# A new order for the attention's software pipeline ahead of two feed-forward blocks on Trainium2

## The chip, the core and the metric

The kernel runs on one core of one Trainium2 chip. The metric is device time in microseconds of one launch, median of three runs. The engines are named as the profile names them: PE (TensorE) with its weight loads PEld, DVE (VectorE), ACT (ScalarE), POOL (GpSimd) and SP (SyncE, which issues nearly all the DMAs).

## What is computed

Sliding-window attention with sink tokens, then two feed-forward blocks, all in float32:

```python
scores = scale * q @ k^T            # batch 2, heads 8, 768 tokens, head_dim 64
keep = (key < n_sink) | ((0 <= query - key) & (query - key < window))   # 4 and 128
a = softmax(where(keep, scores, -1e9))
x = (a @ v) as 1536 x 512
x = ((x @ w_a) * (x @ w_b)) @ w_out          # d_ff 1536
h = maximum(x @ w_in, 0); out = (h * h) @ w_out2   # d_ff 2048
```

The feed-forward weights arrive as 8-byte numbers of which the kernel itself makes float32, and every float32 product of the two blocks is made of three products of rounded parts (high times high, low times high, high times low).

## The kernel before

**Attention.** The work is cut into 24 groups: 2 batches, 6 blocks of 128 queries, 2 halves of 4 heads. A group passes through named stages, which the function `attention_fast` defines: `scores` (PE, L225), `soft0` and `soft1` (DVE, L238 and L241: fold the two key blocks, add the mask, take the extremum), `exp0` and `exp1` (ACT, L249), `rec` (DVE, L254 and L255: reciprocal of the sums), `norm`, `normA`, `normP` (the four heads' scaling, shared by DVE L259, ACT L264, POOL L269), `sp` (POOL, L278 to L280: the sink probabilities split in parts), `pst` and `ptp` (PE transposes, L310 and L286), `st` and `th` (ACT copies out of PSUM), `lu` (POOL, L301 and L303: two triangular parts), `x` (PE, L324 and L329: times the values), `xh` (ACT) and `xl` (DVE, L340), which leave the high and low part of the result in SBUF. A first block of a batch (`i == 0`) has no sinks and no second key block, so its groups are lighter.

The loop runs over 27 steps. In step g the table `ORDER` is gone through from left to right; an entry `(name, lag)` issues stage `name` of group g + lag. All four engines execute what they are given in that order (`manual_schedule`), so the table is each engine's instruction order.

**Beside the attention.** Three kinds of entry belong to the feed-forward part. `abs`, `ts`, `stt`, `stt2`, `cast`, `lo` are the six stages in which one weight matrix of 128 x 512 is decoded (method `Weights.stages`: ACT L511, DVE L515 and L516, DVE L519, DVE L522, ACT L527, DVE L529); the table `DECODE` says in which step the decoding of the j-th matrix starts, the lag of an entry moves its stage to a later step. `fill` issues the 12 PE products of one feed-forward piece (L619), `fu` and `fm` take its result out of PSUM (ACT L632, DVE L636). A piece is issued once 512 tokens of x are finished and, for the first eight, once its weights are decoded. The eight PSUM banks go to the scores (4), to the transposes and x (2), and to two more of the latter until step `WIDE`, when these two become the banks of the feed-forward pieces (pool `ps_a0`).

Ahead of the loop, `warm(WARM0)` issues 14 PE products of a zero matrix (L349), whose results nobody reads. `later_masks` (L116 to L124, six DVE operations) and `flag` (L131 to L136, five small ones, whose result is read after the whole fast path) stand behind step 0.

**After the attention.** The eight pieces that are left run with further decoding, then the pool `ps_a0` is closed and two new pools of four banks each are opened, `ps_y` for the accumulators (L660) and `ps_a` for the inner products (L619), and six phases over the remaining weights follow, each over three blocks of 512 tokens.

Of the kernel before, what the change touches and what calls it, by code (L numbers as in the profile page):

```python
# [16 lines left out]
PSUM = bass.MemoryType.PSUM  # L17
# [8 lines left out]
NRAW, AHEAD = 3, 2  # L26

ORDER = [
# [4 lines left out]
DECODE = [2, 5, 9, 10, 11, 12, 12, 15, 18, 20, 22]  # L33
WIDE = 9
VS = (3, 6)
PINNED = 3
WARM0 = 14
NQ, NV, NEX, NTH, NLU, NSP = 3, 5, 3, 2, 2, 2
NK = 4
T = 512  # L40
# [67 lines left out]
def out_of(v, o, x, limit):  # L108
    v.tensor_scalar(out=o, in0=x, scalar1=limit, scalar2=-BIG, op0=ALU.is_ge, op1=ALU.mult)


def later_masks(tc, cp, tp, c):
    v = tc.nc.vector
    m0, m1, m2 = c.m
    c.up = cp.tile([P, P], I32, name="upi")
    v.tensor_copy(c.up, c.upf)  # L116

    out_of(v, m2[:, 0:P], c.rel, c.w)
    v.tensor_copy(m2[:, P:SW], c.sink[:, 0:SK])

    t = tp.tile([P, P], F32, name="t")
    v.scalar_tensor_tensor(out=t, in0=c.col, scalar=c.ns, in1=c.upf, op0=ALU.is_lt, op1=ALU.mult)
    v.scalar_tensor_tensor(out=m1[:, 0:P], in0=t, scalar=-BIG, in1=m2[:, 0:P], op0=ALU.mult, op1=ALU.min)
    v.tensor_copy(m1[:, P:SW], c.sink[:, 0:SK])  # L124


def flag(tc, cp, c):

    v = tc.nc.vector
    f = cp.tile([P, 4], F32, name="flags")  # L130
    v.tensor_scalar(out=f[:, 0:1], in0=c.ns, scalar1=float(SK), scalar2=None, op0=ALU.is_gt)  # L131
    v.tensor_scalar(out=f[:, 1:2], in0=c.w, scalar1=float(P), scalar2=None, op0=ALU.is_gt)
    v.tensor_scalar(out=f[:, 2:3], in0=c.w, scalar1=1.0, scalar2=None, op0=ALU.is_lt)
    v.reduce_max(out=f[:, 3:4], in_=f[:, 0:3], axis=AX.X)
    c.slow = cp.tile([P, 1], I32, name="slow")
    v.tensor_copy(c.slow, f[:, 3:4])  # L136


def attention_fast(tc, ctx, c, cp, tp, q, k, v, vs_in, xh, xl, beside):
# [16 lines left out]
    def bank(name):  # L156

        turn[0] += 1
        return banks[turn[0] % len(banks)].tile([P, GH, P], F32, name=name, tag="tr")
# [34 lines left out]
    def sink_load(b):  # L194
        vsr[b] = p1.tile([96, H // 2, P], F32, name="vsr", tag="vsr")
        nc.sync.dma_start(vsr[b], vs_in[:, b])
# [30 lines left out]
    def maxima(g, pp):  # L227

        b, i, m = groups[g]
        if pp == 0:  # L230
            pns[g] = (p2.tile([P, GH, SW], F32, name="ex", tag="ex", bufs=NEX),
                      p2.tile([P, GH], F32, name="ss", tag="ss", bufs=NEX),
                      p2.tile([P, GH], F32, name="nb", tag="nb", bufs=NEX))
        ex, ss, nb = pns[g]
        w, at = (P, 0) if i == 0 else (SW, around(g)[1] * SW)
        sc = scs[g][pp]
        if i > 0:
            nc.vector.copy_predicated(sc[:, :, at:at + P], c.up.unsqueeze(1).to_broadcast([P, 2, P]),  # L238
                                      sc[:, :, SW - at:SW - at + P])
        for h in range(2 * pp, 2 * pp + 2):  # L240
            nc.vector.tensor_tensor_reduce(  # L241
                out=ex[:, h, 0:w], in0=sc[:, h % 2, at:at + w], in1=c.m[min(i, 2)][:, 0:w], scale=-0.125,
                scalar=3.0e38, op0=ALU.add, op1=ALU.min, accum_out=nb[:, h:h + 1])
# [100 lines left out]

    def warm(n):

        ps = bank("psw").rearrange("p h t -> p (h t)")[:, 0:2 * P]
        for _ in range(n):
            nc.tensor.matmul(ps, lhsT=beside.zero, rhs=beside.zero[:, 0:1].to_broadcast([P, 2 * P]), start=True,  # L349
                             stop=True)  # L350

    stages = dict(scores=scores, ptp=probs, th=probs_copy, lu=probs_select, soft0=lambda g: maxima(g, 0),
                  soft1=lambda g: maxima(g, 1), exp0=lambda g: exps(g, 0), exp1=lambda g: exps(g, 1), rec=reciprocal,
                  sp=sinks, pst=sinks_turn, st=sinks_copy, x=values, xh=x_high, xl=x_low,
                  norm=normalize, normA=normalize_a, normP=normalize_p)
    warm(WARM0)
    for g in range(N + 3):
        if g == WIDE:
            banks.pop()
            wide.close()  # L360
            beside.open()
        if g % 2 == 0:
            load_kq(g // 2 + 2)
            load_v(g // 2 + 1)
        if g == 0:
            sink_load(0)
        beside.fetch(g)
        for name, lag in ORDER:
            if name in stages:
                if 0 <= g + lag < N:  # L370
                    stages[name](g + lag)
            else:
                beside.stage(name, g + lag)
        if g == 0:
            later_masks(tc, cp, tp, c)
            flag(tc, cp, c)
        if g in VS:
            sink_split(VS.index(g))
            if g == VS[0]:
                sink_load(1)  # L380
# [177 lines left out]
class Beside:  # L558
# [18 lines left out]

    def fetch(self, step):

        if step + 1 in DECODE[:2]:  # L580
            self.W.load()

    def stage(self, name, step):
# [9 lines left out]
        else:  # L593
            for j, at in enumerate(DECODE):
                if at == step:
# [133 lines left out]
@with_exitstack  # L729
def sliding_window_moe_kernel(ctx, tc, q, k, v, vs, span, w_a, w_b, w_out, w_in2, w_out2, out):  # L730
    nc = tc.nc
    NT, DM = out.shape
    cp = ctx.enter_context(tc.tile_pool(name="cp", bufs=1))
    xp = ctx.enter_context(tc.tile_pool(name="xp", bufs=1))
    xh = xp.tile([P, DM // P, NT], F32R, name="xh")
    xl = xp.tile([P, DM // P, NT], F32R, name="xl")
    rp = ctx.enter_context(tc.tile_pool(name="rp", bufs=3))
    sa = ctx.enter_context(tc.tile_pool(name="sa", bufs=1))

    def slots(pool, n):  # L740
        return [(pool.tile([P, 512], F32R, name=f"wh{j}"), pool.tile([P, 512], F32R, name=f"wl{j}")) for j in range(n)]

    first = slots(sa, FIRST)
    zero = cp.tile([P, P], mybir.dt.bfloat16, name="zero")
    nc.vector.memset(zero, 0.0)
    mk = ctx.enter_context(ExitStack())
    tp = mk.enter_context(tc.tile_pool(name="mk", bufs=1, side="right"))
    c = setup(tc, cp, tp, span)

    def run(attend):  # L750
        W = Weights(tc, cp, rp, w_a, w_b, w_out, w_in2, w_out2)
        W.free = list(first)
        F = Ffn(tc, W, xh, xl, xp, out)
        with ExitStack() as c0:
            c0.callback(mk.close)
            wk0 = c0.enter_context(tc.tile_pool(name="wk0", bufs=2, side="right"))
            beside = Beside(tc, W, F, wk0, c0, zero, NT)
            with ExitStack() as c1, tc.manual_schedule(engines=ORDERED):
                attend(c1, beside)
            with tc.tile_pool(name="sb", bufs=1) as sb:  # L760
                W.free += slots(sb, NSLOT)
                for at in beside.work:
                    if at is None:
                        W.ahead()
                c0.close()
                with ExitStack() as c2:
                    ps_y = c2.enter_context(tc.tile_pool(name="ps_y", bufs=4, space=PSUM))
                    ps_a = c2.enter_context(tc.tile_pool(name="ps_a", bufs=4, space=PSUM))
                    wk = c2.enter_context(tc.tile_pool(name="wk", bufs=2))
                    for ph in range(1, len(W.phases)):  # L770
                        for t0 in range(0, NT, T):
                            for _ in F.block(ph, t0, t0 + T == NT, ps_y, ps_a, wk):
                                W.ahead()

    def attend_any(ctx, beside):
        attention_any(tc, c, q, k, v, xh, xl)
        beside.open()

    run(lambda ctx, beside: attention_fast(tc, ctx, c, cp, tp, q, k, v, vs, xh, xl, beside))
    slow = nc.values_load(c.slow[0:1, 0:1], min_val=0, max_val=1,  # L780
                          skip_runtime_bounds_check_because="the flag is 0 or 1")
    with tc.If(slow != 0):
        run(attend_any)
# [68 lines left out]
```

## Time and profile before

| | us |
|---|---|
| median of 3 runs (lowest, highest) | 658.88 (657.35, 659.07) |
| the profiled execution's own time | 660.43 |
| its span, first to last instruction | 658.7 |
| PE busy | 638.1 (97%), 3162 matmuls |
| DVE busy | 384.5 (58%) |
| ACT busy | 279.1 (42%) |
| POOL busy | 59.7 (9%) |
| mean granted clock of PE | 0.989 |

The busy time of PE is made of matmuls whose ends are modelled and which overlap, so 97% doesn't say that each stretch is full. Whether one is, is seen from the waits listed for PE in that stretch and from the distance between starts. The table's two lines on the profiled execution differ by 1.7 us, which lie around the span.

### The profile page before, as it was taken

The numbers are of one execution on the slowest core, as the hardware profiler recorded it, in microseconds if no ns is written. First come the engines' busy times: TensorE is split into PE (matmuls) and PEld (weight loads), VectorE is DVE, ScalarE is ACT, GpSimd is POOL, SyncE is SP. The second block draws the span as 40 slices with busy tenths as digits, with TensorE's granted clock in tenths as the row PEclk, the third lists the DMA queues.
The fourth block names the chain that finished last, engine by engine and source line by source line (L and its number), as shares of the span: only waits on it lengthen the run. The fifth ranks groups of instructions, "written<-read, shape, count | busy, mean of one in ns | idle before, by whom it ended". The sixth has DMA issues, their size and how long they took to land.

```text
span 658.7 us, 8703 instructions
## 1 busy us (share of the span) xinstructions
PE 638.1 (97%) x3162; PEld 515.9 (78%) x3162; DVE 384.5 (58%) x908; ACT 279.1 (42%) x652; POOL 59.7 (9%) x132
## 2 busy tenths in 40 slices
PE   6879999998999999999999999999999999999996
PEld 4557777787888788888888888888888888888885
DVE  6888868536898813989242999327723233232323
ACT  5897767523446414545122554316522222222221
POOL 1565344400000000000000000000000000000000
PEclk8798999999999999999999999999999999999999
DMA  8445412011444500354100242102100000000001
GB/s 290 152 144 170 160 52 66 33 33 55 169 133 155 175 17 1 127 160 162 63 0 1 93 134 94 64 1 64 33 0 1 1 0 1 0 29 36 36 30 69
DMA packets 17411, 49.47 MB, mean 75 GB/s; under 512 B 2064, under 2 KB 2576, under 8 KB 17360
## 3 DMA queue, kind: packets, MB, share of 16 engines
q1 hardware_dynamic: 17216, 48.83, 22.7%
q8 instruction: 27, 0.44, 0.3%
q14 instruction: 24, 0.20, 0.1%
q10 hardware_dynamic: 144, 0.00, 0.0%
HBM read 45.68 MB, written 3.15 MB: 74 GB/s over the span
## 4 chain that ended last, share of the span: by engine, by line
PE 84%; DVE 6%; DMA 4%; ACT 2%; issue 1%; POOL 1%; SPq 1%; POOLq 0%; ACTq 0%; DVEq 0%
PE psa L619 45%; PE acc L660 31%; DMA wraw<-in_moe_w_a_dram 3%; PE sc L225 3%; PE x L324 3%; DMA wraw<-in_moe_w_out_dram 1%; PE ptp L286 1%; DVE wtmp L522 1%; DVE wtmp L519 1%; PE x L329 1%; ACT wtmp L511 1%; ACT ex L249 1%; DVE ex L241 1%; DVE wl L529 1%; DVE gl L59 1%
## 5 line engine op out<-in xcount | busy, mean ns | idle before, releaser
L619 PE MATMUL psa<-xh,wh 128*128 128x512 f32 x480 | 188.1, 392 | 1.8 <-DVE gs L636 1.8
L619 PE MATMUL psa<-xh,wl 128*128 128x512 f32 x480 | 186.9, 389 | 0.0
L619 PE MATMUL psa<-xl,wh 128*128 128x512 f32 x480 | 186.8, 389 | 0.0
L619 PEld LDWEIGHTS psa<-xh,wh 128*128 128x128 f32 x480 | 90.1, 188 | 20.4 <-issue 2.2
L619 PEld LDWEIGHTS psa<-xh,wl 128*128 128x128 f32 x480 | 90.1, 188 | 18.9
L619 PEld LDWEIGHTS psa<-xl,wh 128*128 128x128 f32 x480 | 90.1, 188 | 18.2
L699 DVE TENSOR_TENSOR g<-u 128x512 f32<-128x512 f32 x48 | 33.1, 691 | 112.4 <-ACT u L689 112.4
L689 ACT ACTIVATE u<-psa 128x512 f32<-128x512 f32 x48 | 28.7, 598 | 120.8 <-PE psa L619 120.8
L660 PE MATMUL acc<-wh,gl 128*128 128x512 f32 x192 | 74.7, 389 | 0.0
L660 PE MATMUL acc<-wl,gh 128*128 128x512 f32 x192 | 74.7, 389 | 0.0
L58 ACT CAST gh<-g 128x512 fp32r<-128x512 f32 x72 | 44.7, 620 | 69.3 <-DVE g L696 35.6
L59 DVE TENSOR_TENSOR gl<-g,gh 128x512 fp32r<-128x512 f32 x72 | 49.7, 690 | 31.8 <-ACT gh L58 31.6
L511 ACT ACTIVATE wtmp<-wraw 128x512 f32<-128x512 f32 x68 | 45.5, 673 | 48.9 <-DMA wraw<-in_moe_w_out_dram 11.2
L660 PE MATMUL acc<-wh,gh 128*128 128x512 f32 x192 | 62.7, 389 | 0.0
L527 ACT CAST wh<-wtmp 128x512 fp32r<-128x512 f32 x68 | 42.0, 620 | 40.2 <-DVE wtmp L522 20.0
L660 PE MATMUL acc<-gl,wh 128*128 128x512 f32 x144 | 56.2, 390 | 0.0
L660 PE MATMUL acc<-gh,wl 128*128 128x512 f32 x144 | 56.0, 389 | 0.0
L529 DVE TENSOR_TENSOR wl<-wtmp,wh 128x512 fp32r<-128x512 f32 x68 | 46.4, 685 | 16.2 <-ACT wh L527 15.2
L660 PE MATMUL acc<-gh,wh 128*128 128x512 f32 x144 | 47.9, 391 | 0.2 <-ACT part L719 0.2
L522 DVE SCALAR_TENSOR_TENSOR wtmp<-wraw,wtmp 128x512 int32<-128x512 int32 x68 | 47.7, 704 | 0.2
L519 DVE SCALAR_TENSOR_TENSOR wtmp<-wraw,wtmp 128x512 int32<-128x512 int32 x68 | 46.9, 693 | 0.2
L660 PEld LDWEIGHTS acc<-wl,gh 128*128 128x128 f32 x192 | 36.0, 188 | 7.5
(83 smaller groups left out, 719.9 us busy)
## 6 DMA issues: line engine op xcount, KB each, us to landing
wraw<-in_moe_w_out_dram SPq DMA_DIRECT2D x28, 512.0 KB, 3.5
wraw<-in_moe_w_in_dram SPq DMA_DIRECT2D x16, 512.0 KB, 3.5
wraw<-in_moe_w_a_dram SPq DMA_DIRECT2D x12, 512.0 KB, 3.8
wraw<-in_moe_w_b_dram SPq DMA_DIRECT2D x12, 512.0 KB, 3.5
values<-in_v_dram SPq DMA_DIRECT2D x12, 256.0 KB, 3.7
out_dram<-part SPq DMA_DIRECT2D x12, 256.0 KB, 2.3
keys<-in_k_dram SPq DMA_DIRECT2D x11, 272.0 KB, 3.8
queries<-in_q_dram SPq DMA_DIRECT2D x11, 256.0 KB, 3.9
```

Source lines behind the costliest of these rows:

```text
L58: nc.scalar.copy(hi, src)
L59: (lo_eng or nc.vector).tensor_sub(lo, src, hi.bitcast(F32))
L225: nc.tensor.matmul(o, lhsT=half(queries[n], r)[:, 2 * m + pp], rhs=y, start=True, stop=True)
L511: a = nc.scalar.activation(tf, up.bitcast(F32), AF.Abs)
L519: nc.vector.scalar_tensor_tensor(out=t, in0=up, scalar=0x3FFFFFFF, in1=t, op0=ALU.bitwise_or, op1=ALU.bitwise_and)
L522: nc.vector.scalar_tensor_tensor(out=t, in0=low, scalar=29, in1=t, op0=ALU.logical_shift_right, op1=ALU.bitwise_or)
L527: nc.scalar.copy(hi, tf)
L529: nc.vector.tensor_sub(lo, tf, hi.bitcast(F32))
L619: self.tc.nc.tensor.matmul(ps, lhsT=w[:, kt, :], rhs=x[:, kt, ts], start=n == 0, stop=n == 3 * KT - 1)
L660: mm = nc.tensor.matmul(acc[d], lhsT=a, rhs=b_, start=f == 0 and j == 0, stop=f == NF - 1 and j == 2)
L689: nc.scalar.activation(u, pa, AF.Relu)
L699: nc.vector.tensor_mul(g, u, u)
```

## The change

The order table, the decode steps, the step of the bank exchange, a table of further zero products, the place of the masks and of the flag, the first weight load, and the order in which two PSUM pools are opened:

```diff
@@ tables
 ORDER = [
-    ("exp1", -1), ("scores", 0), ("st", -2), ("rec", -1), ("fm", 0), ("stt", -1), ("norm", -1), ("th", -2),
-    ("stt2", -1), ("normA", -1), ("soft0", 0), ("abs", 0), ("x", -3), ("sp", -1), ("normP", -1), ("pst", -1),
-    ("fu", 0), ("xh", -3), ("cast", -1), ("fill", 0), ("soft1", 0), ("xl", -3), ("lu", -2), ("ptp", -1),
-    ("exp0", 0), ("ts", 0), ("lo", -1)]
-DECODE = [2, 5, 9, 10, 11, 12, 12, 15, 18, 20, 22]
-WIDE = 9
+    ("exp0", -1), ("exp1", -1), ("fm", 0), ("pst", -2), ("rec", -1), ("st", -2), ("fu", 0), ("scores", 0),
+    ("ptp", -2), ("abs", 0), ("th", -2), ("cast", -2), ("x", -3), ("soft0", 0), ("soft1", 0), ("sp", -1),
+    ("norm", -1), ("warm", 0), ("fill", 0), ("normA", -1), ("normP", -1), ("xh", -3), ("xl", -3), ("stt", -1),
+    ("lo", -2), ("ts", 0), ("lu", -2), ("stt2", -1)]
+DECODE = [4, 8, 10, 11, 12, 13, 14, 15, 18, 19, 20]
+WIDE = 10
+WARM = {0: 14, 1: 3, 2: 12, 3: 6, 4: 9}
@@ the loop over the steps
+        elif g == 1:
+            later_masks(tc, cp, tp, c)
+        elif g == 4:
+            flag(tc, cp, c)
         beside.fetch(g)
         for name, lag in ORDER:
-            if name in stages:
+            if name == "warm":
+                warm(WARM.get(g, 0))
+            elif name in stages:
...
-        if g == 0:
-            later_masks(tc, cp, tp, c)
-            flag(tc, cp, c)
@@ Beside.fetch
-        if step + 1 in DECODE[:2]:
+        if step + 2 == DECODE[0]:
             self.W.load()
@@ the pools after the attention
+                    ps_a = c2.enter_context(tc.tile_pool(name="ps_a", bufs=4, space=PSUM))
                     ps_y = c2.enter_context(tc.tile_pool(name="ps_y", bufs=4, space=PSUM))
-                    ps_a = c2.enter_context(tc.tile_pool(name="ps_a", bufs=4, space=PSUM))
```

`warm` also returns at once for a count of zero. The line numbers of the changed program are higher by one in the attention and by six from L511 on.

Three places show what moves. The first is PE in the first steps. `sc` are the scores, `ptp` the transposed probabilities, `psw` the bank that the zero products write, `x` the result. Before:

```order
L225 MATMUL sc<-keys,queries 128x128 x8
L286 MATMUL ptp<-identr,ex 128x128 x4
L225 MATMUL sc<-keys,queries 128x272 x4
L286 MATMUL ptp<-identr,ex 128x128 x4
L225 MATMUL sc<-keys,queries 128x272 x4
L324 MATMUL x<-th,values 64x128 x4
```

Now, at the end of step 2 and in step 3:

```order
L352 LDWEIGHTS zero
L352 MATMUL psw<-zero 128x256
L226 MATMUL sc<-keys,queries 128x272 x4
L287 MATMUL ptp<-identr,ex 128x128 x4
L325 MATMUL x<-th,values 64x128 x4
L352 LDWEIGHTS zero
```

The scores now stand ahead of the transposes of a step, the transposes belong to a group one older than before, and zero products (44 in five steps) stand behind the x of each step.

The second place is DVE between two steps in the middle of a decoding, where `ss` are the sums of the exponentials, `wtmp` the matrix under decoding, `xl` the low part of a result. Before:

```order
L515 TENSOR_SCALAR wtmp<-wtmp 128x512
L516 TENSOR_SCALAR wtmp<-wtmp 128x512
L254 TENSOR_SCALAR ss<-ss 128x4
L255 RECIPROCAL ss<-ss 128x4
L519 SCALAR_TENSOR_TENSOR wtmp<-wraw,wtmp 128x512
L259 TENSOR_SCALAR ex<-ex,ss 128x128
L522 SCALAR_TENSOR_TENSOR wtmp<-wraw,wtmp 128x512
L238 COPY_PREDICATED sc<-upi,sc 128x2x128
```

Now (steps 5 and 6):

```order
L260 TENSOR_SCALAR ex<-ex,ss 128x128
L341 TENSOR_TENSOR xl<-x,xh 128x2x128
L525 SCALAR_TENSOR_TENSOR wtmp<-wraw,wtmp 128x512
L528 SCALAR_TENSOR_TENSOR wtmp<-wraw,wtmp 128x512
L255 TENSOR_SCALAR ss<-ss 128x4
L256 RECIPROCAL ss<-ss 128x4
L239 COPY_PREDICATED sc<-upi,sc 128x2x128
```

Decoding no longer stands between the reciprocal and the next group's extrema but at the end of a step, and takes three steps where it took two.

The third place is PE where the last piece that is computed beside the attention (weights `wh_83`, `wl_84`) ends and the first inner product of the first phase (`wh_93`, `wl_94`) begins, with the engines whose semaphores each instruction waits for. Before:

```order
L619 MATMUL psa<-xh,wh_83 128x512
L619 MATMUL psa<-xl,wh_83 128x512
L619 MATMUL psa<-xh,wl_84 128x512
L619 MATMUL psa<-xh,wh_93 128x512 [waits DVE_49,Activation_49]
L619 MATMUL psa<-xl,wh_93 128x512
L619 MATMUL psa<-xh,wl_94 128x512
```

Now:

```order
L625 MATMUL psa<-xh,wh_83 128x512
L625 MATMUL psa<-xl,wh_83 128x512
L625 MATMUL psa<-xh,wl_84 128x512
L625 MATMUL psa<-xh,wh_93 128x512 [waits Activation_49]
L625 MATMUL psa<-xl,wh_93 128x512
L625 MATMUL psa<-xh,wl_94 128x512 [waits DVE_49]
```

The first product keeps its wait for ACT; a wait for DVE now stands at the first product with the low part of the weights.

## Rows read from the trace of the kernel before

**Rows 1.** Windows of all engines: stretch, length, busy (instructions), PEclk, DMA share, GB/s.
```profile
22.00:28.00 6.00, 5.67 (x38) 4.07 (x40) 4.41 (x24) 4.55 (x19) 4.52 (x10) 0.66 0.29 85
...
46.00:52.00 6.00, 4.44 (x35) 2.88 (x31) 5.75 (x22) 5.05 (x18) 3.89 (x8) 0.83 0.37 132
...
58.00:64.00 6.00, 6.00 (x55) 4.85 (x53) 4.57 (x18) 5.76 (x20) 2.86 (x6) 1.00 0.44 135
...
158.00:210.00 52.00, 50.21 (x222) 41.15 (x221) 46.01 (x89) 26.16 (x45) 0.00 (x0) 1.00 0.45 148
```

**Rows 2.** Waits of PE, 0 to 54 us, first and last of six.
```profile
PE pst L310 <- POOL sp L280: 4.8, 2, 3.5
...
PE sc L225 <- DMA queries<-in_q_dram: 0.5, 1, 0.5
```

**Rows 3.** Timeline of PE and DVE where the first phase begins.
```profile
161.87 0.47 PE L619 MATMUL psa<-xh,wh 128*128 128x512 f32 x1 [1.79 <-DVE gs L636]
...
163.18 0.68 DVE L59 TENSOR_TENSOR gl<-gs,gh 128x512 fp32r<-128x512 f32 x1
```

**Rows 4.** First FFN product, PE's timeline; then PE's pieces of the chain of waits.
```profile
54.11 0.47 PE L619 MATMUL psa<-xh,wh 128*128 128x512 f32 x1
...
50.16 2.12 PE sc L225 x8
...
68.23 1.12 PE sc L225 x8
...
70.74 2.79 PE psa L619 x12
73.97 1.12 PE sc L225 x8
```

**Rows 5.** Timeline of DVE: flag's first operation, then L254, one per step.
```profile
6.91 0.15 DVE L131 TENSOR_SCALAR flags<-par 128x1 f32<-128x1 f32 x1
...
7.47 0.16 DVE L254 TENSOR_SCALAR ss<-ss 128x4 f32<-128x4 f32 x1
...
10.21 0.17 DVE L254 TENSOR_SCALAR ss<-ss 128x4 f32<-128x4 f32 x1 [1.20 <-ACT ex L249]
...
20.84 0.17 DVE L254 TENSOR_SCALAR ss<-ss 128x4 f32<-128x4 f32 x1
...
24.20 0.17 DVE L254 TENSOR_SCALAR ss<-ss 128x4 f32<-128x4 f32 x1 [0.40 <-ACT ex L249]
...
29.26 0.17 DVE L254 TENSOR_SCALAR ss<-ss 128x4 f32<-128x4 f32 x1 [0.35 <-ACT ex L249]
...
34.62 0.17 DVE L254 TENSOR_SCALAR ss<-ss 128x4 f32<-128x4 f32 x1
...
37.97 0.17 DVE L254 TENSOR_SCALAR ss<-ss 128x4 f32<-128x4 f32 x1 [0.40 <-ACT ex L249]
...
50.71 0.16 DVE L254 TENSOR_SCALAR ss<-ss 128x4 f32<-128x4 f32 x1
```

**Rows 6.** Groups by line: the decoding's five operations on DVE.
```profile
L529 DVE TENSOR_TENSOR wl<-wtmp,wh 128x512 fp32r<-128x512 f32 x68 | 46.4, 685 | 16.2 <-ACT wh L527 15.2 <-PE psa L619 0.7
L522 DVE SCALAR_TENSOR_TENSOR wtmp<-wraw,wtmp 128x512 int32<-128x512 int32 x68 | 47.7, 704 | 0.2
L519 DVE SCALAR_TENSOR_TENSOR wtmp<-wraw,wtmp 128x512 int32<-128x512 int32 x68 | 46.9, 693 | 0.2
...
L515 DVE TENSOR_SCALAR wtmp<-wtmp 128x512 f32<-128x512 f32 x68 | 28.9, 426 | 20.2 <-ACT wtmp L511 19.5
...
L516 DVE TENSOR_SCALAR wtmp<-wtmp 128x512 int32<-128x512 int32 x68 | 28.5, 422 | 0.7
```

**Rows 7.** The zero products at the start, PE's timeline.
```profile
1.04 3.17 PE L349 MATMUL psw<-zero 128*128 128x256 bf16 x14 [1.04 <-DVE zero L745]
```

**Rows 8.** Timeline of POOL: one operation alone, and beside a decoding on DVE.
```profile
21.71 0.24 POOL L279 CAST sp<-ex 128x64 fp32r<-128x64 f32 x1
...
30.39 0.73 POOL L279 CAST sp<-ex 128x64 fp32r<-128x64 f32 x1
```

More of the change, by code (lines that the diff above doesn't have):

```diff
@@ L345, in warm @@
     def warm(n):
+        if n == 0:
+            return
         ps = bank("psw").rearrange("p h t -> p (h t)")[:, 0:2 * P]
```

## The prediction, made before the changed kernel was run

> **What bounds the kernel now.** I read the windows first, to see where PE has room. PE is full in every window from 54 us on, with two exceptions, and is not full before [rows 1]. The granted clock says the same: it is 1.00 (2.4 GHz) at 58 us, while the windows at 22 and 46 us have means of 0.66 and 0.83 [rows 1], a mixture of the two levels, 2.4 and 1.2 GHz. Then the waits of PE alone: 12.3 us in six entries up to 54 us [rows 2], none from 54 to 136 us, one of 1.79 us at 160 us [rows 3], and nearly none later. So PE sets the time from its first feed-forward product on, which starts at 54.11 us [rows 4]. The products that stand after it on PE are the same before and after the change, apart from one `pst`, so whatever brings that start forward brings the end forward by as much. Only two things can be won: that start, and the 1.79 us.
>
> **How long a step is.** The first feed-forward piece is issued in step 11 in both versions (512 tokens are finished in step 10). So the question is how long eleven steps take. L254 runs once per step [rows 5]. Without decoding a step is 3.36 us (20.84 to 24.20) or 3.35 us (34.62 to 37.97); the two steps over which a decoding is spread take 10.42 us (24.20 to 34.62), 3.70 us more than two plain ones. Of a plain step DVE waits 0.40 us for ACT's exponentials, so DVE's own load is 2.96 us. On PE a plain step is 5.74 us less 2.79 us of feed-forward, 2.95 us at full clock [rows 4]. No engine is full in a plain step: the old order closes a circle in which the sums wait for four exponentials, the next extrema stand behind the sums on DVE, and the next exponentials behind the extrema. Decoding stands inside this circle (L519 and L522 around L259, ahead of the next extrema).
>
> **The change, part by part.**
>
> *Decoding and order.* Before the first feed-forward product three decodings are finished and two are open; after the change two are finished and two have begun. A decoding is 0.69 + 0.70 + 0.69 + 0.43 + 0.42 = 2.93 us on DVE [rows 6]. The new order puts it at the end of a step, so that it fills DVE's waits, and leaves a step of slack between nearly all stages. I therefore take DVE's load as the length of the steps. L254 of group 1 comes at 10.21 us, and earlier by the flag's five operations ahead of the first L254 (7.47 - 6.91 = 0.56 us) [rows 5], at 9.65 us. The nine steps to L254 of group 10 are 9 x 2.96 = 26.6, two decodings 5.9, the first pair of a third 0.85, two splits of the sink values at 0.69 each (estimate, the shape of L529) 1.4, and the flag 0.56: 35.3 us, which ends at 44.95 us. If DVE could use none of its waits the nine steps would be 9 x 3.36 + 8.7 = 38.9 us. I take 35.3, the near end, because DVE's waits are what the decoding is moved into.
>
> *From there to the first product.* PE's step 11 (scores, transposes, x: 2.95 us) begins when the extrema of group 10 are done, which is ahead of L254; so the first product follows L254 by 0 to 2.95 us, half of it 1.5. Before it was 54.11 - 50.71 = 3.40 us, with the scores at 2.12 us instead of 1.12 because the clock was down [rows 4]. The first product then starts at 46.4 us, **7.7 us earlier**. The late end is 38.9 and 2.95: 51.5 us, 2.6 us earlier. The early end takes 0 us after L254, and starts on a crowded DVE that lie about 0.08 us closer than the durations, over some twenty operations: 43.3 us, 10.8 us earlier.
>
> *Zero products.* 14 at the start take 3.17 us, 0.226 us each [rows 7], with the clock at its lower level; at the upper level half, 0.113 (estimate). The 44 new ones are between 10.0 and 5.0 us of PE. They lie in steps 0 to 4, where PE has the light first-block groups and, up to step 2, no x; step 2 with twelve is at most 2.95 + 1.4 us. I cost them at nothing at the upper level: they stand behind each step's x and ahead of scores that wait for DVE anyway. Their purpose would be the clock; if it stays up, PE's 2.95 us fit into steps of 3.9 us (35.3 / 9). If not, see the first rival.
>
> *Masks and flag.* The masks' six operations keep their place on DVE. The flag is counted above; nobody waits for it before the end of the fast path.
>
> *First weight load, bank exchange.* The load moves behind the loads of keys, queries and values on SP's queue and has two steps until its use. The bank exchange one step later costs nothing, since no piece is issued before step 11.
>
> *PSUM pools.* `ps_a` now lies over banks that the scores used and left long ago, so the first inner product doesn't wait for the last L636. The twelve products and four accumulating ones then end just when the first `gl` arrives (163.18 + 0.68 = 163.86 us) [rows 3]. I take 1.6 us of the 1.79; bounds 0 (the chain of waits from 157 to 215 us runs through the decoding, and could demand it back) and 1.8.
>
> *Sum.* 7.7 + 1.6 = 9.3 us. The profiled execution took 660.43 us (span 658.7), which would be 651.1; it stands 1.55 us above the median of 658.88, so the forecast for the median is **649.6 us**. With all early ends it is 658.9 - 10.8 - 1.8 = 646.3 us, with all late ends 656.3 us.
>
> **The rivals.**
>
> *The clock stays down under the zero products (slower).* If PE runs at 1.2 GHz, a step of it is 5.9 us, 2.0 us more than the 3.9 above, and PE takes DVE's place as the bound. It decides from 9.3 / 2.0 = 4.7 such steps on: fewer leave a gain, eight of the ten would give 649.6 + 16 = 665.6 us. For it: the clock was down more than once before [rows 1]. Against: PE had waits there [rows 2], a PE that is itself the bound has none, and zeros fill the early ones. Chance 0.06.
>
> *The clock falls for two steps,* as it did around 22 us [rows 1]. 649.6 + 4 = 653.6 us. For it: no zeros stand in steps 5 to 10, and PE waits there for POOL and DVE. Chance 0.12.
>
> *DVE, with POOL, becomes the bound from step 10 on.* Six decodings now start in steps 10 to 15, one in each. DVE then has 2.96 + 2.93 + 0.34 (half an L636) = 6.23 us a step, PE 5.74; 0.49 us are lost in each of about five steps, 2.5 us, less in steps 12 and 13 with their light groups. POOL's `sp` operation is 0.24 us alone and 0.73 us beside a decoding [rows 8]; the same on two operations makes about 1 us per decoding, and if half of that comes on the path of `pst` and `x` it is 3 us more. That gives 652 to 655 us, 653.5 in the middle. Against: PE had no wait from 54 to 136 us with five decodings started in steps 9 to 12. Chance 0.15.
> The Trainium skill, page "SBUF — State Buffer", section "Who interferes with whom", says that a DVE operation with two SBUF inputs and a POOL operation that reads SBUF shut one another out for the whole instruction. By that rule the stretching is a lock that also holds DVE back when POOL starts first, and it speaks for this rival; the trace agrees as far as the 0.73 us go.
>
> *The order does nothing.* Steps without decoding stay at 3.36 us, and only the fewer decodings count: the late end, 656.3 us, or 658 if the 1.6 us are demanded back. Chance 0.07.
>
> **How the numbers follow.** Forecast 0.60, the four rivals 0.06, 0.12, 0.15 and 0.07. A measurement of this kernel tells about 0.3% (2 us) from no change. Faster than 656.9: the forecast, the second and third rival and most of the fourth, 0.88; within 2 us 0.06; slower 0.06. The range that holds the time 8 times in 10 is 646.3 to 655: the early ends, and up to the third rival's upper end; it leaves out the slow clock and the fourth rival.
>
> **What would show it.** Right: the first feed-forward product at 45 to 48 us, L254 to L254 at 3.9 us on average up to there, no window with a clock of 0.5 after 5 us, and no wait at the first inner product of the first phase. The second rival shows as scores of 2.1 us in steps 5 to 10, the third as PE waits for DVE's extrema or POOL's `sp` and `lu` between 46 and 90 us. Wrong: PE waits of more than 3 us in all after the first product, or a step above 4.4 us.

## The result and the profile after

The changed kernel takes **652.18 us** in the median (651.52 to 652.78), the kernel before 658.98 us (657.35 to 659.54) in the same runs: ratio 0.9901, 95% interval 0.9881 to 0.9921, a gain of 6.8 us. The forecast was 649.6 us with a range from 646.3 to 655.0.

The profiled execution took 652.25 us. Its page:

```profile
span 650.5 us, 8796 instructions
...
PE 639.2 (98%) x3206; PEld 516.1 (79%) x3206; DVE 384.3 (59%) x908; ACT 278.2 (43%) x652; POOL 54.3 (8%) x132
...
PEclk9999999999999999999999999999999999999998
```

The 44 zero products are the 44 matmuls more. The windows that answer to [rows 1] (columns as there):

```profile
22.00:28.00 6.00, 4.99 (x41) 3.11 (x40) 5.72 (x25) 5.34 (x21) 4.10 (x10) 1.00 0.42 131
...
46.00:52.00 6.00, 6.00 (x47) 4.78 (x48) 5.75 (x28) 5.28 (x18) 3.12 (x9) 1.00 0.39 130
...
158.00:210.00 52.00, 52.00 (x231) 43.04 (x230) 48.78 (x94) 28.01 (x50) 0.00 (x0) 1.00 0.50 165
```

The granted clock is 1.00 in these windows and in all others up to PE's last products. PE is full in the window at 46 us, where it was not before, and in the one at 158 us, where the phases begin. DVE at 22 us has 5.72 us of 6 instead of 4.41. The waits of PE, the first of the stretch up to 54 us and the only one behind the first feed-forward product, answering to [rows 2] and [rows 3]:

```profile
PE pst L311 <- POOL sp L281: 3.0, 6, 0.8
...
PE acc L666 <- DVE gl L60: 0.2, 1, 0.2
```

PE's timeline, the zero products of step 0 and the first feed-forward product [rows 4]; then, from PE's pieces of the chain of waits, the last run of the attention:

```profile
5.02 1.73 PE L352 MATMUL psw<-zero 128*128 128x256 bf16 x14
...
46.18 0.44 PE L625 MATMUL psa<-xh,wh 128*128 128x512 f32 x1
```

```profile
129.22 21.85 PE psa L625 x96
```

And DVE's L255 (L254 before) [rows 5]:

```profile
9.69 0.17 DVE L255 TENSOR_SCALAR ss<-ss 128x4 f32<-128x4 f32 x1 [1.33 <-ACT ex L250]
...
12.85 0.17 DVE L255 TENSOR_SCALAR ss<-ss 128x4 f32<-128x4 f32 x1 [0.80 <-ACT ex L250]
...
25.22 0.16 DVE L255 TENSOR_SCALAR ss<-ss 128x4 f32<-128x4 f32 x1
...
29.72 0.17 DVE L255 TENSOR_SCALAR ss<-ss 128x4 f32<-128x4 f32 x1
...
36.87 0.17 DVE L255 TENSOR_SCALAR ss<-ss 128x4 f32<-128x4 f32 x1 [0.19 <-ACT ex L250]
...
45.67 0.17 DVE L255 TENSOR_SCALAR ss<-ss 128x4 f32<-128x4 f32 x1
```

**Where the time went.** Four marks cut both profiled executions: the first feed-forward product, the start of the last run of 96 feed-forward products that closes the attention, the start of a run of 36 in the middle of the phases, and the end of the span. All runs of this study in these marks (us; x96 and x36 stand for the starts of these two runs, which are read from the chain of waits; each ratio is to runs of the kernel before from the same session, with medians of 658.95 to 660.04 us):

| kernel | first product | from there to x96 | x96 to x36 | x36 to the end | span | median, ratio to before (95%) |
|---|---|---|---|---|---|---|
| before | 54.11 | 81.41 | 195.27 | 327.9 | 658.7 | 658.98 |
| changed | 46.18 | 83.04 | 192.81 | 328.5 | 650.5 | 652.18, 0.9901 |
| e1 new order, old dates | 52.13 | 83.00 | 192.91 | 327.8 | 655.8 | 657.90, 0.9972 (0.9957 to 0.9986) |
| e2 old order, new dates | 50.12 | 82.45 | 194.54 | 327.8 | 654.9 | 656.78, 0.9946 (0.9926 to 0.9967) |
| e3 no zeros in the steps | 46.97 | 83.02 | 192.81 | 327.9 | 650.7 | 652.58, 0.9890 (0.9872 to 0.9907) |
| e4 PE sequence, first try | 49.26 | 95.37 | 192.81 | 327.9 | 665.3 | 667.07, 1.0102 (1.0084 to 1.0119) |
| e5 before, new pools | 52.40 | 81.41 | 194.09 | 327.8 | 655.7 | 657.08, 0.9963 (0.9951 to 0.9975) |
| e6 changed, old pools | 46.12 | 83.02 | 194.34 | 327.7 | 651.2 | 652.96, 0.9905 (0.9890 to 0.9920) |
| e7 before, with zeros | 53.48 | 81.39 | 194.46 | 327.9 | 657.2 | 658.98, 0.9988 (0.9976 to 1.0000) |
| e9 PE sequence, second try | 48.62 | 81.57 | 192.81 | 327.8 | 650.8 | 652.48, 0.9898 (0.9883 to 0.9913) |
| e10 changed, first date old | 50.78 | 83.03 | 192.80 | 327.9 | 654.5 | 655.50, 0.9943 (0.9928 to 0.9957) |
| e11 two orders | 48.29 | 81.53 | 192.85 | 328.1 | 650.8 | 651.35, 0.9869 (0.9850 to 0.9888) |
| e12 less on DVE | 45.90 | 83.02 | 192.79 | 327.7 | 649.4 | 651.26, 0.9872 (0.9853 to 0.9891) |
| e13 e11 and e12 | 46.39 | 81.93 | 192.82 | 328.1 | 649.2 | 651.04, 0.9868 (0.9849 to 0.9887) |

The span is 8.2 us shorter: 7.93 us at the first product, 1.63 us given back up to x96, 2.46 us won from x96 to x36, 0.57 us given back behind x36. All of the last lies behind the start of the run of 36 accumulating products that closes the kernel (14.76 us against 14.0 to 14.4 in all others), so it belongs to that execution.

### The profile page after: what moved, and what is told of

It is laid out like the page before. It is cut to its first block, busy times and chain, and to the rows that moved or that the text cites. A ratio compares the mean times of both kernels' runs of the same rounds, so it can differ in the third digit from the quotient of the medians.

```text
span 650.5 us, 8796 instructions
## 1 busy us (share of the span) xinstructions
PE 639.2 (98%) x3206; PEld 516.1 (79%) x3206; DVE 384.3 (59%) x908; ACT 278.2 (43%) x652; POOL 54.3 (8%) x132
## 4 chain that ended last, share of the span: by engine, by line
PE 94%; DVE 3%; ACT 1%; issue 1%; POOL 0%; DMA 0%; POOLq 0%; ACTq 0%
PE psa L625 50%; PE acc L666 35%; PE sc L226 3%; PE x L325 3%; PE ptp L287 2%; PE x L330 1%; DVE ex L242 1%; PE psw L352 0%; ACT ex L250 0%; DMA keys<-in_k_dram 0%; DVE wtmp L525 0%; PE pst L311 0%; POOL ex L279 0%; DVE wtmp L528 0%; DVE vs L201 0%
## 5 line engine op out<-in xcount | busy, mean ns | idle before, releaser
L666 PEld LDWEIGHTS acc<-wh,gh 128*128 128x128 f32 x192 | 36.1, 188 | 7.5
```

Of the source, the lines that this page charges most:

```text
L666: mm = nc.tensor.matmul(acc[d], lhsT=a, rhs=b_, start=f == 0 and j == 0, stop=f == NF - 1 and j == 2)
```

## Experiments

### Order and dates apart (e1, e2, e10)

e1 takes the dates and the load's place of before into the changed kernel; e2 takes the new ones into the kernel before, by the reverse edit (with its 12 twice).

```diff
-DECODE = [4, 8, 10, 11, 12, 13, 14, 15, 18, 19, 20]
+DECODE = [2, 5, 9, 10, 11, 12, 13, 15, 18, 20, 22]
...
-        if step + 2 == DECODE[0]:
+        if step + 1 in DECODE[:2]:
```

> The changed kernel with the old decode steps and the old place of the weight load (the old table has two decodings in step 12; one of them moves to 13 here, which lies behind the first feed-forward product). Theory of the prediction (order and decode steps each give a part, DVE's load is the length of a step): by L254 of group 10 DVE has done 0.69 + 0.70 + 0.85 = 2.2 us more of decoding than in the changed kernel, so the first feed-forward product moves from 46.2 to 48.4 us and the time from 652.2 to 654.4 us. Rival (the order gives nothing, the decode steps give all): first product near 54 us, time 659.0 less the 1.6 us of the pools = 657.4 us. Rival (the order gives all): 652.2 us.

> The kernel before with the new decode steps and the new place of the weight load alone; order, zero products, pools, masks and flag as before. Theory of the prediction: one decoding less ahead of the first feed-forward product, which in the old order lengthened two steps by 3.70 us: first product 54.1 - 3.7 = 50.4 us, time 659.0 - 3.7 = 655.3 us; plain steps stay at 3.36 us. Rival (the decode steps give all but the pools' 1.6 us): first product near 46 us, time 652.2 + 1.6 = 653.8 us. Rival (they give nothing): 659.0 us.

Measured: the first product comes 3.99 us earlier by the dates alone (e2), 1.98 us earlier by the rest of the change (e1), 7.93 us by both. The theory of the prediction met e2 (50.12 against 50.4 forecast) and missed e1 by 3.7 us (52.13 against 48.4): the new order needs the new dates. The 1.98 us of e1 are no more than two executions of one program can differ by: e5 below, whose program is that of before up to there, has its first product at 52.40 us instead of 54.11. By its time, 657.90 us, e1 lies at its first rival's 657.4, that the order alone gives little beyond the pools. The time of e2, 656.78 us, is 1.5 us above its forecast: from the first product to x96 it takes 1.04 us more than the kernel before, and PE waits there for POOL's `sp` for 0.9 us. ACT's timeline of e1 shows why the order needs the dates, with a row that also the kernel before has. There first, then e1:

```profile
13.22 0.68 ACT L511 ACTIVATE wtmp<-wraw 128x512 f32<-128x512 f32 x1 [1.83 <-DMA wraw<-in_moe_w_a_dram]
```

```profile
13.08 0.66 ACT L517 ACTIVATE wtmp<-wraw 128x512 f32<-128x512 f32 x1 [3.18 <-DMA wraw<-in_moe_w_a_dram]
```

ACT stands before the first weight matrix, which comes behind the keys, queries and values: the DMA share from 4 to 16 us is 1.03 in the kernel before and 0.98 in e1. e10 takes this alone:

```diff
-DECODE = [4, 8, 10, 11, 12, 13, 14, 15, 18, 19, 20]
+DECODE = [2, 8, 10, 11, 12, 13, 14, 15, 18, 19, 20]
```

> The changed kernel with the first decoding started in step 2 as before the change (its load issued in step 0), all other dates as changed; two decodings are finished ahead of the first feed-forward product in both. Theory A (part of the gain is that ACT, which works in order, no longer stands waiting for the first weights behind the keys, queries and values, 1.83 us in the kernel before and 3.18 us in the new order with the old dates): ACT waits about 3 us for the weights near 13 us, L254 of group 3 comes 3 us later, first product at about 48 to 49 us, time 654.5 to 655.5 us. Theory B (only the number of decodings ahead of the first product counts): 652.2 us.

Theory A holds, with a larger effect than it expected (first product at 50.78 us, not 48 to 49). The timeline of ACT in e10, then DVE's L255 of group 2:

```profile
13.07 0.66 ACT L517 ACTIVATE wtmp<-wraw 128x512 f32<-128x512 f32 x1 [3.55 <-DMA wraw<-in_moe_w_a_dram]
...
14.69 0.40 ACT L250 ACTIVATE ex<-ex,nb 128x136 f32<-128x136 f32 x1
```

```profile
16.39 0.17 DVE L255 TENSOR_SCALAR ss<-ss 128x4 f32<-128x4 f32 x1 [1.74 <-ACT ex L250]
```

The next exponentials come behind the wait, and so L255 of group 2 comes 3.5 us later than in the changed kernel (16.39 against 12.85). Another 1.3 us are lost in the step behind it, in which the granted clock is 0.65 and then 0.50 (windows of 2 us from 14 to 18 us). At the first product it is 4.60 us, more than half of what the change won there, and 3.3 us of the median, with as many decodings finished ahead of it as in the changed kernel. So it is the date of the first decoding, not the number of decodings, that carries most. The Trainium skill, page "PSUM — Partial Sum Buffer", section "Engine vs sequencer instructions", says that ScalarE's queue is strictly first in, first out; the rows agree, since ACT starts nothing between its operation of 9.33 us and that of 13.07 us.

### Zero products (e3, e7)

e3 is the changed kernel with

```diff
-WARM = {0: 14, 1: 3, 2: 12, 3: 6, 4: 9}
+WARM = {}
```

and e7 the kernel before with that table, the two lines of the loop that read it, and

```diff
-    ("fu", 0), ("xh", -3), ("cast", -1), ("fill", 0), ("soft1", 0), ("xl", -3), ("lu", -2), ("ptp", -1),
+    ("fu", 0), ("xh", -3), ("cast", -1), ("warm", 0), ("fill", 0), ("soft1", 0), ("xl", -3), ("lu", -2), ("ptp", -1),
```

> The changed kernel without the 44 zero products inside the steps (the 14 ahead of the loop stay). Costing of the prediction (they lie beside DVE's work and take no time) with a clock that stays up by the order alone: 652.2 us, first feed-forward product at 46.2 us, granted clock 1.00 in all windows from 6 us on. Rival (the zero products are what holds the clock): windows between 6 and 40 us with a granted clock of 0.5 to 0.8, two to four steps in which PE takes 2.0 us more, time 656 to 660 us. Rival (the zero products are on the path): up to 44 x 0.12 = 5.3 us earlier, 647 us.

> The kernel before with the 44 zero products alone, 14, 3, 12, 6 and 9 of them in steps 0 to 4 behind x. Theory (the zeros hold the clock, and the granted clock is a small part of the gain): no window below 0.9 between 6 and 22 us, the fall around 22 us may stay since no zeros stand there; time 0.5 to 1.5 us under the kernel before, ratio 0.998 to 0.999. Rival (they are on the path of a PE whose clock is low): 44 x 0.1 to 0.2 us, 1 to 5 us slower.

Windows of e3, then of the kernel before, then of e7 (columns as in [rows 1]):

```profile
10.00:12.00 2.00, 0.73 (x4) 0.33 (x4) 1.93 (x12) 1.99 (x8) 0.60 (x1) 1.00 1.05 330
12.00:16.00 4.00, 3.93 (x21) 2.44 (x23) 2.68 (x15) 2.39 (x9) 1.31 (x4) 0.57 1.04 402
```

```profile
14.00:18.00 4.00, 0.46 (x7) 0.27 (x4) 3.11 (x11) 3.50 (x13) 1.83 (x4) 1.00 0.92 354
18.00:26.00 8.00, 7.29 (x37) 4.22 (x38) 7.04 (x35) 7.35 (x27) 3.85 (x11) 0.58 0.53 166
```

```profile
14.00:18.00 4.00, 0.93 (x12) 0.73 (x9) 3.15 (x12) 3.42 (x14) 2.09 (x4) 1.00 1.03 394
18.00:22.00 4.00, 4.00 (x24) 2.44 (x23) 3.69 (x17) 3.19 (x13) 0.98 (x4) 0.57 0.70 264
```

Each time the mean clock is near the lower level (1.2 GHz) in the stretch behind one in which PE had little to do. Without the zeros of the steps this happens once in the new order, at 12 us, and costs 0.79 us at the first product; the median is 0.4 us higher, less than the spread of the runs. All seven profiles that have the zeros, the new order or a variant of it, and the new dates show 1.00 from 6 to 44 us, so the zeros seem to hold the clock there, though only one profile lacks them; the rival overpriced it at two to four slow steps. In the old order they cannot fill the hole at 14 us, since PE itself waits there for POOL's `sp` (3.1 us), which is taken, untested, to be late by ACT's wait; e7 won 0.12%, with an interval (0 to 0.24%) that reaches zero. Its clock was not as expected: the low stretch behind 18 us stayed.

### The pools (e5, e6)

```diff
-                    ps_y = c2.enter_context(tc.tile_pool(name="ps_y", bufs=4, space=PSUM))
                     ps_a = c2.enter_context(tc.tile_pool(name="ps_a", bufs=4, space=PSUM))
+                    ps_y = c2.enter_context(tc.tile_pool(name="ps_y", bufs=4, space=PSUM))
```

This is e5, in the kernel before; e6 is the reverse edit in the changed kernel.

> The kernel before with only the two PSUM pools opened in the other order. Theory of the prediction: the first inner product of the first phase loses its wait of 1.79 us, 1.6 us of it are won to the end, ratio 0.9976. Rival (the chain behind it, decoding and accumulators, demands it back): ratio 1.000, with waits of PE between 161 and 215 us.

> The changed kernel with the two PSUM pools in their old order. Theory: the wait of 1.8 us at the first inner product of the first phase is back and the time 1.6 us longer, 653.8 us. Rival: the decoding in the changed kernel is further ahead, so the wait is hidden or shorter, 652.2 us.

The waits of PE at the first phase, of e6 and then of e5:

```profile
PE psa L625 <- DVE gs L642: 1.8, 1, 1.8
```

```profile
PE acc L660 <- ACT gh L58: 0.9, 1, 0.9
PE acc L660 <- DVE gl L59: 0.2, 1, 0.2
```

In the new order the pools are worth 194.34 - 192.81 = 1.53 us of the stretch from x96 to x36, as the theory has it. The medians differ by 0.8 us only, with intervals that overlap; the changed kernel's profile carries the 0.57 us of its long end. In the old order 0.9 us come back at once as a wait for ACT, and that stretch is 0.4 us shorter than in e7, which has the old pools (194.09 against 194.46): the rival was right there in part. The 0.37% (2.4 us) of e5 are more than that stretch shows: its first product came at 52.40 us instead of 54.11, in a part of the program that is the same as before. There the clock differs: from 6 to 16 us its mean is 1.00 in e5 and 0.83 before, from 22 to 26 us 1.00 and 0.50. The two steps of a decoding that the prediction read as 10.42 us (24.20 to 34.62) take 9.20 us in e5, whose L254 has:

```profile
23.71 0.17 DVE L254 TENSOR_SCALAR ss<-ss 128x4 f32<-128x4 f32 x1 [0.40 <-ACT ex L249]
...
32.91 0.17 DVE L254 TENSOR_SCALAR ss<-ss 128x4 f32<-128x4 f32 x1
```

### The sequence on PE (e4, e9, e11)

The 1.63 us that were given back: no wait of PE is listed in that stretch, yet a full step is longer. PE's timeline of one step, its twelve feed-forward products shown by the first, in the kernel before and in the changed one:

```profile
86.71 0.47 PE L619 MATMUL psa<-xh,wh 128*128 128x512 f32 x1
...
89.52 0.60 PE L286 MATMUL ptp<-identr,ex 128*128 128x128 f32 x4
90.05 1.19 PE L225 MATMUL sc<-keys,queries 64*128 64x272 f32 x8
91.17 1.09 PE L324 MATMUL x<-lu,values 128*64 128x128 f32 x16
92.19 0.44 PE L329 MATMUL x<-st,vs 96*128 96x128 f32 x2
92.47 0.23 PE L310 MATMUL pst<-identr,sp 128*96 128x128 f32 x1
92.53 0.46 PE L619 MATMUL psa<-xh,wh 128*128 128x512 f32 x1
```

```profile
79.56 0.44 PE L625 MATMUL psa<-xh,wh 128*128 128x512 f32 x1
...
82.37 0.22 PE L311 MATMUL pst<-identr,sp 128*96 128x128 f32 x1
82.53 1.19 PE L226 MATMUL sc<-keys,queries 64*128 64x272 f32 x8
83.64 0.66 PE L287 MATMUL ptp<-identr,ex 128*128 128x128 f32 x4
84.23 1.09 PE L325 MATMUL x<-lu,values 128*64 128x128 f32 x16
85.25 0.44 PE L330 MATMUL x<-st,vs 96*128 96x128 f32 x2
85.53 0.45 PE L625 MATMUL psa<-xh,wh 128*128 128x512 f32 x1
```

From `psa` to `psa` it is 5.82 us before and 5.97 us now. Start to start, `pst` takes 0.06 us ahead of `psa` and 0.16 us ahead of `sc`; `ptp` takes 0.53 us ahead of `sc` and 0.59 us ahead of `x`. Together that is 0.16 us, which accounts for the 0.15 us of a step; why a transpose takes longer ahead of one product than ahead of another no run here shows. e4 put both back where they stood, with the ACT copies `st` and `th` behind them:

```diff
-    ("exp0", -1), ("exp1", -1), ("fm", 0), ("pst", -2), ("rec", -1), ("st", -2), ("fu", 0), ("scores", 0),
-    ("ptp", -2), ("abs", 0), ("th", -2), ("cast", -2), ("x", -3), ("soft0", 0), ("soft1", 0), ("sp", -1),
-    ("norm", -1), ("warm", 0), ("fill", 0), ("normA", -1), ("normP", -1), ("xh", -3), ("xl", -3), ("stt", -1),
+    ("exp0", -1), ("exp1", -1), ("fm", 0), ("rec", -1), ("fu", 0), ("scores", 0),
+    ("abs", 0), ("cast", -2), ("x", -3), ("pst", -2), ("st", -2), ("soft0", 0), ("soft1", 0), ("sp", -1),
+    ("norm", -1), ("warm", 0), ("fill", 0), ("normA", -1), ("normP", -1), ("xh", -3), ("xl", -3), ("ptp", -2), ("th", -2), ("stt", -1),
```

> The changed kernel with the old sequence on PE inside a step: scores, x, pst, feed-forward, ptp in place of pst, scores, ptp, x, feed-forward; the ACT copies st and th move along. Theory: the steps in which PE is full take 5.97 us in the changed kernel and took 5.83 before, because pst in front of the scores and ptp between scores and x cost 0.09 and 0.06 us more of PE each step; with the old sequence about 14 such steps get 0.14 us shorter, the x96 run of psa comes 2.0 us earlier against the first product, time 650.2 us. Rival (the longer steps come from something else, the other engines' traffic): 652.2 us with steps of 5.97 us. Rival (th and lu come late for x of the next step): PE waits for POOL's lu, over 653 us.

Measured 667.07 us, the last rival: `ptp` at the end of a step leaves its copy and POOL's `lu` no time before the next `x`. The waits of PE of e4 from 54 to 140 us:

```profile
PE x L325 <- POOL lu L302: 8.1, 12, 1.4
```

The second try, e9, puts `ptp` ahead of the scores and `pst` behind `x`, with `st` behind `xh`, so that the sequence is the old one and `ptp` stays a step ahead (these lines take the place of the same three of the changed kernel):

```diff
+    ("exp0", -1), ("exp1", -1), ("fm", 0), ("ptp", -2), ("rec", -1), ("fu", 0), ("scores", 0),
+    ("abs", 0), ("th", -2), ("cast", -2), ("x", -3), ("pst", -2), ("soft0", 0), ("soft1", 0), ("sp", -1),
+    ("norm", -1), ("warm", 0), ("fill", 0), ("normA", -1), ("normP", -1), ("xh", -3), ("st", -2), ("xl", -3), ("stt", -1),
```

> The changed kernel with ptp ahead of the scores and pst behind x, so that PE runs ptp, scores, x, pst, feed-forward inside a step as the kernel before did, while ptp stays a step ahead of its x (in the earlier try it stood behind the feed-forward and x waited for POOL's lu). Theory: steps with PE full take 5.83 us as before and not 5.97, the first feed-forward product to the x96 run of psa takes 1.6 us less, time 650.4 us if the first product stays at 46.2 us. Rival (the longer steps are not of the sequence on PE): steps of 5.97 us, 652.2 us. Rival (ptp ahead of the scores holds the scores back while DVE sets the step): first product later by up to 10 x 0.6 us, time up to 656 us.

Both the theory and the second rival came true. The stretch from the first product to x96 is 81.57 us, 1.47 us shorter, with steps of 5.86 us (81.31 to 87.17). But the first product came 2.44 us later, since `ptp`, which waits for DVE's `norm`, now holds the scores back while DVE sets the step. The longest of PE's waits of e9 up to 48 us:

```profile
PE ptp L287 <- DVE ex L260: 5.4, 6, 1.3
```

The time is the same, 652.48 us. e11 therefore takes this order, as a table `FULL`, from step 11 on only:

```diff
-        for name, lag in ORDER:
+        for name, lag in ORDER if g < 11 else FULL:
```

> The changed kernel, but from step 11 on (where the feed-forward pieces begin and PE is full) with the order in which ptp stands ahead of the scores and pst behind x; up to step 10 the changed kernel's order. Theory (the sequence on PE makes the 5.97 us): first product at 46.2 us as in the changed kernel, first to last piece 81.4 us instead of 82.9 us, time 652.2 - 1.5 = 650.7 us. Rival (changing the order at step 11 makes a wait, ptp ahead of the scores holds them back): first product later by up to 2.4 us, 652 us or more.

The stretch is again 81.5 us, and the first product again late, by 2.11 us. The exchange of the orders makes a wait in step 11. Timeline of PE and two windows of e11 (columns as in [rows 1]), then the same of e13, which has the same wait:

```profile
43.68 0.63 PE L292 MATMUL ptp<-identr,ex 128*128 128x128 f32 x4 [2.04 <-ACT ex L255]
```

```profile
44.00:46.00 2.00, 2.00 (x13) 1.06 (x13) 1.93 (x6) 1.30 (x4) 0.22 (x2) 0.70 0.22 82
46.00:48.00 2.00, 2.00 (x17) 1.67 (x18) 1.78 (x10) 0.47 (x2) 1.85 (x6) 0.50 0.51 149
```

```profile
43.35 0.63 PE L292 MATMUL ptp<-identr,ex 128*128 128x128 f32 x4 [2.04 <-ACT ex L255]
```

```profile
44.00:46.00 2.00, 2.00 (x24) 1.45 (x24) 1.79 (x7) 1.31 (x4) 0.44 (x2) 1.00 0.07 24
```

In this execution of e11 the clock fell behind the wait, in that of e13 it did not: from `ptp` to the first product it is 4.61 us in e11 (43.68 to 48.29) and 3.04 us in e13 (43.35 to 46.39). So 1.57 of the 2.11 us are the low clock and only about 0.5 us the wait itself. The other executions of e11 were up to 1.6 us faster than the profiled one (650.84 against 652.46). A change of order one or two steps later was not tried.

### Less on DVE ahead of the first product (e12), and all together (e13)

```diff
-        elif g == 4:
+        elif g == 12:
             flag(tc, cp, c)
...
-VS = (3, 6)
+VS = (3, 12)
```

> The changed kernel with the five flag operations moved from step 4 to step 12 and the second split of the sink values (0.68 us on DVE, 0.62 us on ACT) from step 6 to step 12. Theory of the prediction (up to the first feed-forward product DVE's load is the length of a step): 0.56 + 0.69 = 1.25 us less load in the first ten steps, L254 of group 10 at 44.4 and the first product at 44.9 us, time 652.2 - 1.2 = 651.0 us. Rival (the steps there are set by something else, a circle over ACT or POOL): first product at 46.2 us, 652.2 us.

L255 of groups 1, 2 and 10 in e12:

```profile
10.19 0.17 DVE L255 TENSOR_SCALAR ss<-ss 128x4 f32<-128x4 f32 x1 [0.88 <-ACT ex L250]
...
13.33 0.17 DVE L255 TENSOR_SCALAR ss<-ss 128x4 f32<-128x4 f32 x1 [0.77 <-ACT ex L250]
...
45.40 0.16 DVE L255 TENSOR_SCALAR ss<-ss 128x4 f32<-128x4 f32 x1
```

From group 1 to group 10 it is 35.21 us instead of 35.98 (35.22 in e13, which has the same edit): 0.77 us of the 1.25 us that DVE has less to do. Part of the rest shows as DVE's waits for ACT's exponentials within these steps, 1.84 us (0.77 above, then 0.57 and 0.50) against 0.99 in the changed kernel. So DVE's load sets most of the length, not all. The edit takes 0.62 us off ACT too, and ACT is as full as DVE there (busy 33.24 us of the changed kernel's 35.98; DVE 32.79, PE 32.91), so e12 alone doesn't tell the two apart; that DVE waits for ACT for only 0.99 us does speak for DVE.

At the first product only 0.28 us are left, because group 1 began 0.5 us late: the zero products of step 0 took 2.41 us in this execution, on the chain of waits, and 1.73 us in the changed kernel's. The granted clock is listed as 1.00 in both, so that it came up later is inferred from the lengths alone. The timeline of PE:

```profile
5.30 2.41 PE L352 MATMUL psw<-zero 128*128 128x256 bf16 x14
```

> The two edits together: the second order from step 11 on, and flag and second split in step 12. If both theories hold they add, since one shortens the steps ahead of the first product and the other those behind it: first product at 44.9 us, first to last piece 81.4 us, time 652.2 - 1.5 - 1.2 = 649.5 us. Rival: ptp ahead of the scores in a step 12 that DVE now has more of gives part of it back, 650.5 us or more.

Measured 651.04 us: first product at 46.39 us with the wait of step 11, 81.93 us from there to x96, 0.4 us more than in e11. The rival expected such a loss in step 12; it came later, from 70.89 to 76.39 us, where a step takes 5.50 us (5.17 in e11) and `ptp` waits 0.17 us for DVE. By the medians e12, e11 and e13 are 0.9, 0.8 and 1.1 us faster than the changed kernel; their intervals overlap its own, so none is shown to beat it by a measurable amount. All three beat the kernel before.

## Why the prediction was right, and where it was not

**The bound and the first product.** That PE sets the time from its first feed-forward product on held, and this start was forecast at 46.4 us and came at 46.18 us. Its parts: L255 of group 1 at 9.69 (9.65 forecast), nine steps of 35.98 us in all (35.3), 0.51 us to the product (1.5). The last two miss by 0.7 and 1.0 us and cancel, so that the start agrees within 0.2 us is in part luck. The steps are 4.00 us on average; the longest, 4.50 us (25.22 to 29.72), is 0.1 us above the 4.4 that the prediction named as a sign of being wrong. DVE's load as the length of a step is borne out by DVE's 5.5 to 5.7 us of 6 in the windows from 16 to 46 us and by its waits of 0.99 us in all nine steps; e12 met the forecast of 1.25 us by only 0.77 us, and ACT is next to being the bound.

**The reason for the old steps was incomplete.** The prediction put the long steps of the old order down to the decoding that stands in its circle, and gave the first weight load no price ("has two steps until its use"). e10 shows that the date of the first decoding alone is worth 4.60 us at the first product: the row of ACT that waits 1.83 us for the first weights stood in the profile of before and was not read. Besides, 1.2 of the 3.70 us by which a decoding lengthened two old steps are missing in e5 (9.20 us instead of 10.42), where the clock did not fall. The number agreed because the new start was built up from DVE's load and not from what made the old steps longer.

**The step that failed** is "whatever brings that start forward brings the end forward by as much". The same products in another sequence took 0.15 us more per step, 1.63 us in all; e9 and e11 take 1.47 and 1.51 us of that away by the sequence (the ACT copy `st` moves along), which shows the cause.

**The correction to the median** was the other miss. The sum was 9.3 us from a profiled execution of 660.43 us, which gives 651.1; the profile after is 652.25, 1.1 us more: 1.63 of the sequence and 0.57 of the end, less 0.23 at the first product and 0.86 from x96 to x36. The further 1.55 us, by which that execution stood above its median, were subtracted as if the changed kernel's would too. But the excess lay in part where the change works: e5 and e7, the same as before in that stretch or with the zeros alone, reach the first product at 52.40 and 53.48 us instead of 54.11. The changed kernel's execution stands 0.07 us above its median.

**Pools.** 1.6 us were forecast; e6 puts them at 1.53 us. The other 0.9 us of the 2.46 us won from x96 to x36 belong mostly to the execution of before: e2 and e7 with the old pools take 194.5 us there, it took 195.27 us.

**Zero products** cost 0.12 us each (1.73 us for 14; 0.113 forecast) and nothing on the changed kernel's path, as costed. In e12, where the 14 of step 0 took 2.41 us, they delayed group 1 by 0.5 us. That the 14 ahead of the loop ran at the lower level is read from their 0.226 us each; the granted clock is listed as 1.00 there.

**The rivals.** The clock stayed up, so the two clock rivals did not come; e3 has a small form of the second, 0.8 us instead of 4. DVE and POOL did not become the bound: PE waits for POOL not at all behind its first product and for DVE 0.2 us, and POOL's operation of [rows 8] is no longer stretched. Its group, from the groups by line:

```profile
L280 POOL CAST sp<-ex 128x64 fp32r<-128x64 f32 x20 | 4.8, 238 | 1.3
```

Its mean of 238 ns is the 0.24 us of the operation alone. That the order does nothing falls with e2: the new dates in the old order bring the first product to 50.12 us, 3.94 us behind the changed kernel. Of the chances, 0.88 for a measurable gain counts only 0.01 of this rival's 0.07, where the prediction says most of it.

**What was not taken apart.** The bank exchange one step later and the masks' new place were run only together with the rest.

## What to carry to other kernels

An engine that works in order makes everything behind a late operand late: before pricing a moved stage, look at what the engines wait for in the first steps, the DMA's landing among them, and move the stage past the wait. Once PE is the bound, the sequence of its own products is a cost of its own, seen in the distance between starts and in no wait; an order that suits the stretch where another engine sets the step need not suit the stretch where PE does. And where a profiled execution lies above its median, ask in which stretch before correcting for it.

## What the runs showed of the chip that was not expected

The same PE products differ by 0.15 us per step of 5.8 us with their sequence, with no wait listed. The clock fell to the lower level behind 4 us in which PE was busy for 0.46 us (before), but behind a wait of 2.04 us it fell in one execution (e11) and not in another (e13), which made 1.57 us up to the first product. Between the kernel before and e5, the same program up to there, such falls go with 1.71 us. The zero products of step 0, ahead of all this, took 1.73 or 2.41 us with the same program up to there.
